# A residual quantiser with depthwise convolutions: three small operations of a stage go from VectorE to GpSimd, score tiles hold eight groups in shared PSUM tiles, and DMA transposes and adding DMAs take strict turns

## The chip, the cores and the metric

The kernel runs on one core of a Trainium2 chip. The metric is the device time of one execution in microseconds (us). The engines are named as in the profile: PE (TensorE), DVE (VectorE), ACT (ScalarE), POOL (GpSimd) and SP (SyncE, which here only issues transfers). A "q" behind the name (POOLq, SPq) means the engine's instruction queue issuing a transfer or waiting.

## The reference

The input x has 2 sequences of 16000 tokens with 512 channels, in bf16. A depthwise convolution with three taps and a SiLU give z. Four rounds of residual quantisation follow, each with a code book of 8 words, and the sum of the chosen words goes through a second depthwise convolution.

```python
for i in range(K):                      # K = 3 taps
    z = z + xp[:, i:i+T, :] * dw_enc[i]
z = silu(z)
res, q = z, 0
for s in range(4):                      # four code books of 8 words
    cb = codebooks[s]
    d2 = sum(res*res)[..., None] - 2.0 * einsum("btd,cd->btc", res, cb) + sum(cb*cb)
    sel = cb[d2.argmin(-1)]
    q, res = q + sel, res - sel
for i in range(K):
    y = y + qp[:, i:i+T, :] * dw_dec[i]
```

## The kernel before

The 32000 tokens are laid out as 128 partitions by 250 groups: group g holds one token of each partition. The groups are worked on in 16 chunks (`SIZES`: one of 12, fourteen of 16, one of 14, which is padded to 16). Channels lie on the partitions in four blocks of 128, tokens along the free dimension.

**Loading.** The rows of chunk 0 come in with a plain transfer (L291) into the third residual buffer, PE transposes them into `ps_x` (L454), and ACT and DVE move two blocks each to `XT` (L459, L461). All later chunks come in with DMA transposes issued by SP, up to four groups each (L486). `XT` has two buffers.

**Front** (`front`, four blocks a chunk): DVE makes the three tap products Z and T (L553). They are added on DVE (L561) or, for most, by a DMA that POOL issues and that adds T onto Z on its way (L559, 75 of them). SiLU takes an exponential (L565), plus one on DVE (L569), a logarithm (L573), another exponential (L576), all three on ACT, and a product on DVE (L581) that writes the residual tile RES.

**Four stages** (`stage`), each in this order:
- PE writes a mask (L637) and then the products of RES with itself and with the code words (L643) into a PSUM score tile. In the kernel before a tile `PS` is one bank with up to six groups, from a pool `psG` of two.
- DVE takes each token's squared norm out of the tile with a maximum (L651, `norm`) and copies the dots with the eight words (L654, `dots`).
- DVE adds the norm (L673, `with_norm`), adds the words' own norms (L679, `distance`) and puts a rank into the low half of each key so that the first of equal words wins (L684, `ranks`).
- DVE takes the least key (L689) and makes a one-hot pattern (L697). PE transposes it (L707), and DVE copies it out (L714).
- Except in the last stage, the chosen word is taken off the residual in eight parts: on PE and DVE (`SEL` L731, L747) or on PE and ACT (`NEW` L752 and L731, L758). How many of the four channel blocks go to DVE in stages 0, 1 and 2 stands in `ON_DVE`; each block is two parts.

**Output** (`finish`, `outputs`): the decoder is a product of one-hot patterns with tables of words times taps (`Y`, L785); ACT copies it out (L791) and SP stores it (L795).

The other PSUM tiles (`ps_oh`, `SEL`, `NEW`, `Y`) come from a pool `psA` of three tiles with two banks each. The three residual buffers, key buffers and one-hot buffers set how many chunks are under way.

**Order.** The order of the instructions is made by a planner (`Plan`): each task has an engine, a time for which it holds that engine, a time until its result is there, needs, a due time and the buffers it takes and gives. `ROUNDS` holds seeds and numbers of forward and backward passes. Tasks are written out in the order of their planned starts, so each engine's queue follows the plan and runs strictly in that order. Into planned idle time of PE the planner puts matmuls without use (`warm`, L430; `WARM` is the share of busy time it aims for), which keep PE's clock up. Transposes and adding DMAs have the planner's engine "DMA". In the program, `keep_apart` makes each wait for an earlier one of the other kind:

```python
if len(others) >= LAG:
    tc.add_manual_dep(t.ins, others[-LAG].name, ...)
```

The adds' wait stands in POOL's queue, the transposes' in SP's.

Of the kernel before, what the change touches and what calls it, by code (L numbers as in the profile page):

```python
# [21 lines left out]
GB = 6  # L22
# [6 lines left out]
ON_DVE = [(1, 2, 2)]  # L29
# [3 lines left out]
WARM = 0.6  # L33
# [4 lines left out]

RUN = 4

AHEAD = 40

# [4 lines left out]
ROUNDS = [(940, 0.3, 0.0, 7), (4101, 0.3, 2.0, 9), (5991, 0.3, 0.0, 7), (15520, 0.3, 0.0, 10)]  # L47
# [6 lines left out]
APART, CLUMP = 0.5, 2.0  # L54

LAG = 2


class Plan:
# [18 lines left out]
    def pass_over(self, rank, backward=False):  # L78
# [20 lines left out]
        while True:  # L99
            going = True  # L100
            while going:
                going = False
                for e in engines:
# [3 lines left out]
                    while e == "DMA" and ready[e]:  # L107
                        at, n = heapq.heappop(ready[e])
                        passed.append((at, n))
                        if all(slots[k] > 0 for k in tasks[n][takes]):  # L110
                            kind, lost = tasks[n][8][0], 0.0
                            if kind and sort and kind != sort:
                                lost = max(0.0, APART - (now - ended))
                            if pick is None or at + CLUMP * lost < least:
                                pick, least, gap = n, at + CLUMP * lost, lost
# [62 lines left out]
    def emit(self, starts, order):  # L178
        tasks = self.tasks
        free, back, spans, end = self.slots["psG"], [], [], 0.0  # L180
        for n in order:
            engine, hold, delay, _, _, emit, take, give, _, _ = tasks[n]
            at = starts[n]
            if engine == "PE":
                while end + 0.3 <= at:
# [3 lines left out]
                    while spans and spans[0][1] < end - 4.0:  # L189
                        spans.pop(0)  # L190
                    if free > 0 and sum(b - max(a, end - 4.0) for a, b in spans) < 4.0 * WARM and self.idle():
                        spans.append((end, end + 0.3))
                        end += 0.3
                    else:
                        end += 0.1
# [5 lines left out]
            free -= take.count("psG")  # L201
            for _ in range(give.count("psG")):
                heapq.heappush(back, at + max(hold, delay))
# [4 lines left out]
def kernel(  # L208
# [32 lines left out]
    psG = ctx.enter_context(tc.tile_pool(name="psG", bufs=2, space=bass.MemoryType.PSUM))  # L241
    psA = ctx.enter_context(tc.tile_pool(name="psA", bufs=3, space=bass.MemoryType.PSUM))
# [25 lines left out]
    def tap_columns():  # L268
        pst = psA.tile([P, 2, 512], F32, name="ps_w", tag="psa")
# [6 lines left out]
    plan = Plan({"XT": 2, "Z": ZB, "T": TB, "E": EB, "LN": LNB, "Y": YB, "psG": 2, "psA": 3, "RES": 3, "KEY": 3,  # L276
# [14 lines left out]
    nc.sync.dma_start(out=XR[:, 1:G + 2, :], in_=xv[:, 0:G + 1, :])  # L291
    for b in range(B):
        p = b * HB
        nc.scalar.dma_start(out=XR[p + 1:p + HB, 0, :], in_=xv[p:p + HB - 1, S - 1, :])
# [4 lines left out]
    def code_words():  # L299
        pst = psA.tile([P, 2, 512], F32, name="ps_cbt", tag="psa")  # L300
# [13 lines left out]
    def code_norms():  # L314
# [12 lines left out]
        psg = psA.tile([P, 2, 512], F32, name="ps_g", tag="psa")  # L327
# [69 lines left out]
    ident, book = landed(1.8), landed(9.3)  # L397
    taps_in = setup(0.2, 0.4, [ident, landed(3.0)], early, tap_columns)
# [24 lines left out]
    pending = []  # L423

    def warm():
        if not scored[2:]:
            return False
        if not pending:
            pending.append(psG.tile([P, 512], F32, name="PS"))
        nc.tensor.matmul(pending[0][:, 0:GB * HT].rearrange("p (r c) -> p r c", c=HT), lhsT=IDENT, rhs=MASK, start=True, stop=True,  # L430
                         skip_group_check=True)
# [4 lines left out]
    def ahead():  # L436
        pending.append(psG.tile([P, 512], F32, name="PS"))
        for _ in range(AHEAD):
            nc.tensor.matmul(pending[0][:, 0:P], lhsT=IDENT, rhs=IDENT, start=True, stop=True, skip_group_check=True)

    plan.add("PE", 0.1 * AHEAD, 0.1 * AHEAD, [taps_in], early, ahead)

    def load_rows(st, org):
# [6 lines left out]
        def turn(i):  # L450
            pst = psA.tile([P, 2, 512], F32, name="ps_x", tag="psa")
            st["ps", i] = pst.rearrange("p b n -> p (b n)").bitcast(BF16)
            for n in range(G + 2):
                nc.tensor.transpose(st["ps", i][:, n * P:(n + 1) * P], XR[:, n, i * P:(i + 1) * P], IDENT)  # L454

        def move(i):
            src = st["ps", i][:, 0:(G + 2) * P].rearrange("p (n t) -> p n t", t=P)
            if i % 2:
# [4 lines left out]
        rows = st["rows"] = plan.add("LOAD", 0.0, 1.2 + 0.46 * (G + 2), [], early, room, take=("XT",))  # L463
        for i in range(KT):
            t = plan.add("PE", 0.11 * (G + 2), 0.11 * (G + 2) + 0.2, [rows, ident], early, lambda i=i: turn(i),
                         take=("psA",))
            cost = (0.11, 0.07)[i % 2] * (G + 2)
            st["moved", i] = plan.add(("ACT", "DVE")[i % 2], cost, cost + 0.2, [t], early, lambda i=i: move(i), give=("psA",))
# [4 lines left out]
    def load(st, org):  # L473
# [29 lines left out]
        def behind():  # L503
            nc.gpsimd.tensor_copy(st["XT"][0:1, 0, 0, 0:2], XR[0:1, 1, 0:2])
# [10 lines left out]
        for n in range(0, G + 2, RUN):  # L515
            due = org - 2.2 * PERIOD + 0.01 * n
            m = min(RUN, inside - n)
            if m > 0:
                done.append(plan.add("DMA", 0.7 * m, 2.7 + 0.7 * m, [room], due, lambda n=n, m=m: run(n, m), mode=RUNS))
# [94 lines left out]
    def stage(st, s, due):  # L614
# [14 lines left out]
        def score(q, m):  # L629
# [4 lines left out]
            PS = pending.pop() if pending else psG.tile([P, 512], F32, name="PS")  # L634
            V = u["V", q] = PS[:, 0:m * (hi - lo)].rearrange("p (r c) -> p r c", r=m)
            for h in range(2):
                nc.tensor.matmul(V[h * HT:(h + 1) * HT, :, own:own + HT], lhsT=IDENT[:, h * HT:(h + 1) * HT], rhs=MASK[:, 0:m, :],  # L637
                                 start=True, stop=False, skip_group_check=True)
            for r in range(m):
                for i in range(KT):  # L640
                    for h in range(2):
                        half = RES[:, i, 2 * (q + r) + h, :]
                        nc.tensor.matmul(V[h * HT:(h + 1) * HT, r, :], lhsT=half[:, LC:LC + HT], rhs=half[:, lo:hi],  # L643
# [6 lines left out]
        def norm(q, m):  # L650
            nc.vector.tensor_reduce(out=u["TR"][:, q:q + m], in_=u["V", q][:, :, own:own + HT], axis=AX.X, op=ALU.max)  # L651

        def dots(q, m):
            nc.vector.tensor_copy(u["PR"][:, q:q + m, :], u["V", q][:, :, pick:pick + C])  # L654

        banks = -(-G // GB)
        q = 0
        for n in range(banks):
            m = -(-(G - q) // (banks - n))
# [4 lines left out]
            t = plan.add("PE", 0.175 * m, 0.175 * m + 0.25, needs, due, lambda q=q, m=m: score(q, m), take=("psG",), mode=(COLUMNS, COLUMNS, 0, 0.0),  # L664
# [3 lines left out]
            maxima.append(plan.add("DVE", 0.06 + 0.01 * m, 0.2, [maxima[-1]], due, lambda q=q, m=m: dots(q, m), give=("psG",)))  # L668
            q += m

        def with_norm():
            u["V"] = small.tile([P, GC, C], BF16, name="V")
            nc.vector.tensor_tensor(out=u["V"][:, 0:G, :], in0=u["PR"][:, 0:G, :], in1=u["TR"][:, 0:G].to_broadcast([P, G, C]),  # L673
                                    op=ALU.add)

        def distance():
            u["KEY"] = free["KEY"].pop(0)
            g2 = GPOS[:, C * s:C * s + C].rearrange("p (o c) -> p o c", o=1).to_broadcast([P, G, C])
            nc.vector.tensor_tensor(out=u["KEY"][1][:, 0:G, :, 1], in0=u["V"][:, 0:G, :], in1=g2, op=ALU.add)  # L679

        def ranks():

            word = u["KEY"][1]
            nc.vector.scalar_tensor_tensor(out=word[:, 0:G, :, 0], in0=word[:, 0:G, :, 1], scalar=0.0,  # L684
# [17 lines left out]
        def turn():  # L702

            pst = psA.tile([P, 2, 512], F32, name="ps_oh", tag="psa")
# [13 lines left out]
        t = plan.add("DVE", 0.2, 0.33, maxima, due, with_norm)  # L718
        t = plan.add("DVE", 0.2, 0.33, [t] + preset[0:3], due, distance, take=("KEY",))
        t = plan.add("DVE", 0.2, 0.33, [t], due, ranks)  # L720
# [19 lines left out]
        def chosen(i, j):  # L740
            SEL = u["SEL", i, j] = psA.tile([P, 2, 512], F32, name="SEL", tag="psa")
# [7 lines left out]
        def rest(i, j):  # L749
            NEW = u["NEW", i, j] = psA.tile([P, 2, 512], F32, name="NEW", tag="psa")  # L750
# [22 lines left out]

    kept = {}

    def outputs(groups, needs, due):
# [4 lines left out]
        def decode(k):  # L781
            Y = u[k] = psA.tile([P, 2, D], F32, name="Y", tag="psa")
# [107 lines left out]
```

## Time and profile before

| | |
|---|---|
| time, median of 3 runs | 745.02 us (744.42 to 745.52) |
| the profiled execution | 742.04 us |
| its span | 740.3 us |
| mean granted clock of PE | 0.934 |
| busiest engines | DVE 93%, ACT 90%, PE 80% of the span |
| POOL | 11% of the span |
| DMA queues, share of 16 engines | 39.5% (issued by SP and ACT), 29.9% (by POOL) |

The span runs from the program's first instruction to the end of its last; the rest of the profiled execution's time lies around it. Busy times are of one execution. A group's mean is the duration of one instruction; where instructions of an engine overlap, the next one starts before the mean has passed. "Idle before" is the time in which the engine waited for such an instruction, and the name behind the arrow is what ended most of it.

### The profile page before, as it was taken

Reading aid. Unit: us, or ns where it says so; the run is one execution under the profiler, and the core shown is the slowest. Engines: PE = TensorE matmul, PEld = TensorE weight load, DVE = VectorE, ACT = ScalarE, POOL = GpSimd, SP = SyncE. Lnnn points to the kernel's source line nnn. Section 1 sums busy time; section 2 is a strip of 40 time slices with the busy share of each in tenths; the row PEclk is TensorE's granted clock in tenths of the full one; section 3 lists DMA queues with packets and bytes.
Section 4 is the critical chain, followed back from the end, with each engine's and each line's share of the span. In section 5 each row is a group of like instructions: output and inputs, shape, how many; then the busy total and the mean of one; then the engine's idle time right before and its main releaser. Section 6 shows DMA issues by size and latency. Waiting matters only on the chain. (4 is left out here: it accounts for less than half of the span.)

```text
span 740.3 us, 23586 instructions
## 1 busy us (share of the span) xinstructions
PE 590.8 (80%) x10478; PEld 314.2 (42%) x10544; DVE 685.9 (93%) x1359; ACT 665.4 (90%) x539; POOL 81.7 (11%) x104
## 2 busy tenths in 40 slices
PE   5037687787987888986978888878988898989996
PEld 5023334344444444434444444444453444444543
DVE  6999989899999999997999999989999999998952
ACT  2688979899999999998899999989999999976576
POOL 3112101111101011100101111100111101100000
PEclk9566969999999999999799899999999999999999
DMA  7969795859696967839978875959896435320234
GB/s 178 189 130 182 135 200 104 141 122 201 182 174 158 209 133 164 165 116 143 188 171 177 175 165 143 182 132 174 172 210 136 131 64 152 87 88 2 88 143 199
DMA packets 160833, 111.14 MB, mean 150 GB/s; under 512 B 142426, under 2 KB 142811, under 8 KB 160603
## 3 DMA queue, kind: packets, MB, share of 16 engines
q1 hardware_dynamic: 148976, 69.61, 39.5%
q0 software_dynamic: 11472, 39.76, 29.9%
q8 instruction: 82, 1.34, 0.8%
q10 hardware_dynamic: 282, 0.26, 0.1%
q14 instruction: 21, 0.16, 0.1%
HBM read 2.39 MB, written 32.77 MB: 47 GB/s over the span
## 5 line engine op out<-in xcount | busy, mean ns | idle before, releaser
L758 ACT ACTIVATE RES<-NEW 128x1024 bf16<-128x1024 f32 (+1 forms) x218 | 218.5, 1043 | 28.6 <-PE NEW L731 21.9
L747 DVE TENSOR_TENSOR RES<-RES,SEL 128x1024 bf16<-128x1024 bf16 (+1 forms) x166 | 197.5, 1203 | 6.7 <-PE SEL L731 6.3
L643 PE MATMUL PS<-RES 128*64 128x80 bf16 (+1 forms) x8064 | 176.1, 203 | 11.2 <-DVE RES L581 9.7
L643 PEld LDWEIGHTS <-RES 128*64 128x64 bf16 x8064 | 172.8, 115 | 19.6 <-DVE RES L581 10.6
L752 PE MATMUL NEW<-RES,IDENT 128*128 128x512 bf16 (+1 forms) x436 | 137.7, 399 | 31.3 <-ACT RES L758 15.6
L791 ACT ACTIVATE YSB<-Y 128x1024 bf16<-128x1024 f32 (+1 forms) x126 | 126.6, 1061 | 8.4 <-PE Y L785 4.5
L565 ACT ACTIVATE E<-Z 128x2048 bf16<-128x2048 bf16 (+1 forms) x64 | 123.2, 1931 | 11.5 <-DMA Z<-T 4.0
L559 POOL DMA_DIRECT2D Z<-T x75 | 72.9, 976 | 537.5 <-ACT RES L758 78.8
L573 ACT ACTIVATE LN<-E 128x2048 f32<-128x2048 bf16 (+1 forms) x64 | 123.0, 1923 | 9.9 <-DVE E L569 9.2
L576 ACT ACTIVATE E<-LN 128x2048 bf16<-128x2048 f32 (+1 forms) x64 | 123.0, 1922 | 0.4
L651 DVE TENSOR_REDUCE TR<-PS 128x5 bf16<-128x320 f32 (+1 forms) x188 | 96.0, 515 | 14.4 <-PE PS L643 14.3
L553 DVE TENSOR_SCALAR T<-XT,WENC 128x2048 bf16<-128x2048 bf16 (+1 forms) x128 | 94.8, 745 | 5.1 <-DMA Z<-T 5.1
L731 PEld LDWEIGHTS <-CBN 32*128 32x128 bf16 x768 | 32.6, 92 | 137.7 <-issue 134.3
L785 PE MATMUL Y<-A,OHT 128*128 128x512 bf16 x219 | 77.6, 382 | 16.4 <-ACT RES L758 6.0
L731 PE MATMUL NEW<-OHT,CBN 32*128 32x512 bf16 (+1 forms) x436 | 88.3, 402 | 0.1
L581 DVE TENSOR_TENSOR RES<-Z,E 128x2048 bf16<-128x2048 bf16 (+1 forms) x64 | 77.3, 1208 | 0.0
L731 PE MATMUL SEL<-OHT,CBN 32*128 32x512 bf16 (+1 forms) x332 | 58.7, 396 | 22.0 <-ACT RES L758 13.3
L637 PE MATMUL PS<-MASK,IDENT 128*64 128x320 bf16 (+1 forms) x376 | 64.6, 340 | 8.6 <-DVE PR L654 6.2
L561 DVE TENSOR_TENSOR Z<-Z,T 128x2048 bf16<-128x2048 bf16 (+1 forms) x53 | 62.5, 1181 | 2.7 <-DMA Z<-T 2.7
L752 PEld LDWEIGHTS <-IDENT 128*128 128x128 bf16 x436 | 33.1, 99 | 67.4 <-issue 57.4
L430 PE MATMUL PS<-MASK,IDENT 128*128 128x384 bf16 x167 | 46.2, 359 | 10.1 <-DVE PR L654 9.8
L785 PEld LDWEIGHTS <-OHT 128*128 128x128 bf16 x373 | 32.1, 97 | 50.8 <-issue 22.8
(78 smaller groups left out, 416.2 us busy)
## 6 DMA issues: line engine op xcount, KB each, us to landing
Z<-T POOLq DMA_DIRECT2D x75, 512.0 KB, 5.6
out_dram<-YSB SPq DMA_DIRECT2D x61, 512.0 KB, 3.2
RES<-in_x_dram SPq DMA_DIRECT2D x1, 1664.0 KB, 6.8
XT<-in_x_dram SPq DMA_TRANSPOSE x74, 5.7
out_dram<-YSB SPq DMA_DIRECT2D x1, 384.0 KB, 2.3
out_dram<-YSB SPq DMA_DIRECT2D x1, 256.0 KB, 2.7
A<-in_dw_dec_dram POOLq DMA_DIRECT2D x2, 96.0 KB, 6.4
CB<-in_codebooks_dram ACTq DMA_DIRECT2D x1, 128.0 KB
```

Of the source, the lines that this page charges most:

```text
L553: nc.vector.tensor_scalar(out=places(u[name]), in0=taps(i, k), scalar1=WENC[:, i, k:k + 1], scalar2=None, op0=ALU.mult)
L565: nc.scalar.activation(u["E"][:, 0:G, :], u["Z"][:, 0:G, :], ACT.Exp, scale=-1.0)
L573: nc.scalar.activation(u["LN"][:, 0:G, :], u["E"][:, 0:G, :], ACT.Ln)
L576: nc.scalar.activation(u["E"][:, 0:G, :], u["LN"][:, 0:G, :], ACT.Exp, scale=-1.0)
L643: nc.tensor.matmul(V[h * HT:(h + 1) * HT, r, :], lhsT=half[:, LC:LC + HT], rhs=half[:, lo:hi], start=False, stop=(i == KT - 1), skip_group ...
L651: nc.vector.tensor_reduce(out=u["TR"][:, q:q + m], in_=u["V", q][:, :, own:own + HT], axis=AX.X, op=ALU.max)
L731: nc.tensor.matmul(ps, lhsT=CBN[s][rows, i * P:(i + 1) * P], rhs=u["OHT"][rows, 0:MB, :], start=start, stop=True, skip_group_check=True)
L747: nc.vector.tensor_tensor(out=old, in0=old, in1=u["SEL", i, j][:, :, 0:W].rearrange("p h (m t) -> p h m t", t=HT), op=ALU.add)
L752: nc.tensor.matmul(NEW[:, h, 0:W], lhsT=IDENT, rhs=tokens(i, j + h, 1), start=True, stop=False, skip_group_check=True)
L758: nc.scalar.activation(old, u["NEW", i, j][:, :, 0:W].rearrange("p h (m t) -> p h m t", t=HT), ACT.Copy)
L785: nc.tensor.matmul(Y[:, h, :], lhsT=lhs(), rhs=rhs, start=(a == 0), stop=(a == len(terms) - 1))
L791: nc.scalar.activation(u["YSB"][:, k:k + n, :], u[k][:, 0:n, :], ACT.Copy)
```

## The change

Seven things change together.

1. `with_norm`, `distance` and `ranks` go to POOL in all four stages. `ranks` becomes two instructions there.
2. `GB` goes from 6 to 4, counted for one bank; a score tile is now a double tile of two banks with up to eight groups, written and read as `[:, b, ...]`. The pool `psG` is gone: `psA` has four double tiles, which all users take through `bank`.
3. `ON_DVE` takes turns between (2, 2, 2) and (1, 2, 2).
4. `LAG` is 1: a transpose waits for the last add before it, and an add for the last transpose. The planner's gap between kinds goes from 0.5 to 1.9 or 2.3 us.
5. At the start, the rows of chunk 0 come in with two transfers, all from SP's queue, and PE's transposes of a block go in two parts; one block is moved by DVE and three by ACT. The matmuls ahead of the work (`ahead`) no longer wait for the taps.
6. The warm-up matmuls have 512 columns of code words, use a `psA` tile, and come only ahead of a task that takes such a tile; the planner's parameters for them change.
7. The planner's estimates and seeds (`ROUNDS`) are new, so the order differs everywhere. In the built program DVE has 180 subtractions L747 for 166, 128 reductions and 128 copies of dots for 188 each; ACT has 204 updates for 218; PE has 85 warm-up matmuls for 167. Transposes and adds change places 65 times for 53. POOL has 256 more instructions.

Line numbers are those of the kernel before.

```diff
-GB = 6
+GB = 4
-ON_DVE = [(1, 2, 2)]
+ON_DVE = [(2, 2, 2), (1, 2, 2)]
-WARM = 0.6
+WARM, WINDOW, TICK = 0.75, 3.4, 0.22
+ON_POOL = (0, 1, 2, 3)
+POOL_SMALL = (0.45, 0.65)
-ROUNDS = [(940, 0.3, 0.0, 7), (4101, 0.3, 2.0, 9), (5991, 0.3, 0.0, 7), (15520, 0.3, 0.0, 10)]
+ROUNDS = [(734, 1.0, 0.0, 9), (2861, 0.3, 0.0, 2), (4622, 0.3, 0.0, 3)]
-APART, CLUMP = 0.5, 2.0
-LAG = 2
+APART = (0.0, 1.9, 2.3)
+CLUMP = 2.0
+LAG = 1
...
-    psG = ctx.enter_context(tc.tile_pool(name="psG", bufs=2, space=bass.MemoryType.PSUM))
-    psA = ctx.enter_context(tc.tile_pool(name="psA", bufs=3, space=bass.MemoryType.PSUM))
+    psA = ctx.enter_context(tc.tile_pool(name="psA", bufs=4, space=bass.MemoryType.PSUM))
+    pending = []
+    def bank(name):
+        return pending.pop() if pending else psA.tile([P, 2, 512], F32, name=name, tag="psa")
...
-    nc.sync.dma_start(out=XR[:, 1:G + 2, :], in_=xv[:, 0:G + 1, :])
     for b in range(B):
         p = b * HB
-        nc.scalar.dma_start(out=XR[p + 1:p + HB, 0, :], in_=xv[p:p + HB - 1, S - 1, :])
+        nc.sync.dma_start(out=XR[p + 1:p + HB, 0, :], in_=xv[p:p + HB - 1, S - 1, :])
+    HALF = (G + 2) // 2
+    for a, b in ((1, HALF), (HALF, G + 2)):
+        nc.sync.dma_start(out=XR[:, a:b, :], in_=xv[:, a - 1:b - 1, :])
...
     def warm():
...
-        nc.tensor.matmul(pending[0][:, 0:GB * HT].rearrange("p (r c) -> p r c", c=HT), lhsT=IDENT, rhs=MASK, ...)
+        nc.tensor.matmul(pending[0][:, 0, :], lhsT=IDENT, rhs=CB4, ...)
...
     def score(q, m):
...
-            V = u["V", q] = PS[:, 0:m * (hi - lo)].rearrange("p (r c) -> p r c", r=m)
-            for h in range(2):
-                nc.tensor.matmul(V[h * HT:(h + 1) * HT, :, own:own + HT], lhsT=IDENT[:, h * HT:(h + 1) * HT], rhs=MASK[:, 0:m, :],
-                                 start=True, stop=False, skip_group_check=True)
+            V = u["V", q] = PS[:, :, 0:m // 2 * (hi - lo)].rearrange("p b (r c) -> p b r c", c=hi - lo)
+            for b in range(2):
+                for h in range(2):
+                    nc.tensor.matmul(V[h * HT:(h + 1) * HT, b, :, own:own + HT], lhsT=IDENT[:, h * HT:(h + 1) * HT],
+                                     rhs=MASK[:, 0:m // 2, :], start=True, stop=False, skip_group_check=True)
...
-        banks = -(-G // GB)
+        banks = -(-G // (2 * GB))
...
     def with_norm():
-            nc.vector.tensor_tensor(out=u["V"][:, 0:G, :], in0=u["PR"][:, 0:G, :], in1=u["TR"][:, 0:G].to_broadcast([P, G, C]),
+            small_on(s).tensor_tensor(out=u["V"][:, 0:G, :], in0=u["PR"][:, 0:G, :], in1=u["TR"][:, 0:G].to_broadcast([P, G, C]),
...
     def distance():
-            nc.vector.tensor_tensor(out=u["KEY"][1][:, 0:G, :, 1], in0=u["V"][:, 0:G, :], in1=g2, op=ALU.add)
+            small_on(s).tensor_tensor(out=u["KEY"][1][:, 0:G, :, 1], in0=u["V"][:, 0:G, :], in1=g2, op=ALU.add)
...
     def ranks():
             word = u["KEY"][1]
+            if s in ON_POOL:
+                nc.gpsimd.tensor_scalar(out=u["V"][:, 0:G, :], in0=word[:, 0:G, :, 1], scalar1=0.0, scalar2=None, op0=ALU.is_lt)
+                nc.gpsimd.tensor_tensor(out=word[:, 0:G, :, 0], in0=u["V"][:, 0:G, :], in1=RANK.to_broadcast([P, G, C]), op=ALU.subtract)
+                return
...
+    def small_on(s):
+        return nc.gpsimd if s in ON_POOL else nc.vector
```

102 lines of the change are left out of this document (52 added, 50 removed).

## The prediction

> **What bounds the kernel now.** I began with the page's first part and the busy time of each engine by stretch, because a kernel with a pipeline of 16 chunks has a filling, a steady and an emptying part with different limits.
>
> ```profile
> PE 590.8 (80%) x10478; PEld 314.2 (42%) x10544; DVE 685.9 (93%) x1359; ACT 665.4 (90%) x539; POOL 81.7 (11%) x104
> ```
>
> ```profile
> 100.00:200.00 100.00, 82.18 (x1533) 42.20 (x1538) 94.85 (x185) 94.66 (x76) 11.68 (x12) 0.95 0.78 154
> 200.00:300.00 100.00, 83.38 (x1537) 43.53 (x1544) 99.43 (x196) 99.94 (x81) 10.33 (x11) 0.99 0.80 170
> 300.00:400.00 100.00, 84.31 (x1486) 44.18 (x1496) 94.24 (x186) 93.96 (x77) 10.69 (x12) 0.94 0.79 156
> ...
> 660.00:680.00 20.00, 19.09 (x373) 9.45 (x365) 17.97 (x35) 11.61 (x12) 0.00 (x0) 1.00 0.08 29
> ```
>
> The columns are the stretch, its length, then busy us (and instructions) of PE, PEld, DVE, ACT and POOL, the granted TensorE clock, the DMA share and GB/s. From 100 to 640 us (six rows, three shown) DVE is busy 522.8 and ACT 522.0 of 540 us, both 97%: two engines bound the middle together, and relieving one alone gains nothing. POOL does 11%. From 0 to 60 us ACT is only 60% busy while DVE is full from 20 us on (19.4 and 19.8 of 20): DVE sets the start. From 660 us on PE is at 95%: the emptying part belongs to PE and to the chain through one chunk's stages.
>
> Next, the groups by form, for prices.
>
> ```profile
> L758 ACT ACTIVATE RES<-NEW 128x1024 bf16<-128x1024 f32 x204 | 207.6, 1060 | 27.4 <-PE NEW L731 20.8 <-PE SEL L731 6.5
> L747 DVE TENSOR_TENSOR RES<-RES,SEL 128x1024 bf16<-128x1024 bf16 x156 | 188.4, 1219 | 6.4 <-PE SEL L731 6.3
> L651 DVE TENSOR_REDUCE TR<-PS 128x5 bf16<-128x320 f32 x120 | 58.6, 492 | 8.2 <-PE PS L643 8.1
> L651 DVE TENSOR_REDUCE TR<-PS 128x6 bf16<-128x384 f32 x68 | 37.8, 556 | 6.3 <-PE PS L643 6.2
> L679 DVE TENSOR_TENSOR KEY<-V,GPOS 128x128 bf16<-128x128 bf16 x60 | 18.2, 304 | 0.2
> L684 DVE SCALAR_TENSOR_TENSOR KEY<-KEY,RANK 128x128 bf16<-128x128 bf16 x60 | 18.2, 303 | 0.2
> L673 DVE TENSOR_TENSOR V<-PR,TR 128x128 bf16<-128x128 bf16 x60 | 17.5, 291 | 0.2
> ```
>
> These means are too large as prices on a full engine, since each instruction starts before the last has ended. DVE's timeline shows it (start, duration):
>
> ```profile
> 317.81 0.31 DVE L679 TENSOR_TENSOR KEY<-V,GPOS 128x128 bf16<-128x128 bf16 x1
> 318.00 0.50 DVE L651 TENSOR_REDUCE TR<-PS 128x5 bf16<-128x320 f32 x1
> 318.40 0.31 DVE L684 SCALAR_TENSOR_TENSOR KEY<-KEY,RANK 128x128 bf16<-128x128 bf16 x1
> 318.60 0.77 DVE L553 TENSOR_SCALAR T<-XT,WENC 128x2048 bf16<-128x2048 bf16 x1
> ```
>
> From start to start a small operation takes 0.20 us, not 0.30, and a five-group reduction 0.40. Read the same way, a six-group reduction takes 0.46, a copy of its dots 0.11 to 0.12, a subtraction L747 1.13, and an ACT update L758 0.91.
>
> **The change part by part.** The sum is made against the profiled execution: 742.04 us, a span of 740.3 and 1.7 around it. The median of the runs, 745.02, is 3.0 above it.
>
> *Small operations to POOL.* L673, L679 and L684 leave DVE in all 64 stages: 64 x 3 x 0.20 = 38.4 us. POOL gets four instructions for them (the compare and subtract become two). POOL has no such two-input operation in this trace. Nearest rows: the copy L496 of 508 columns takes 610 ns, a copy of two columns (L504) 174, so 0.86 ns per column: one input of 128 columns costs 0.28 us, and a second input at most as much per column again, 0.39. I take 3 x 0.39 + 0.28 = 1.45, with three handovers 1.6 us (bounds 1.1 to 3.0). That is 64 x 1.6 = 102 us on an engine with 82. In the middle it hides: from the start of L673 to the start of L689 DVE now takes 3.2 us at the median of 64 stages, because other work stands between. Where only one chunk is left, the three take 1.0 us (725.75 to 726.75 in the chain), so there it adds 0.6 a stage.
>
> *Eight groups to a score tile.* Sixty stages of 16 groups go from tiles of 6, 5 and 5 to two of 8. Per 64 columns a reduction costs 0.067 more, so 512 columns take 0.60. Before: 0.46 + 2 x 0.40 + 0.34 for three copies = 1.60; after: 2 x (0.60 + 0.13) = 1.46. That saves 60 x 0.14 = 8.4 us of DVE. PE's masks go from six of 0.13 to 0.16 to eight of 256 columns, about even.
>
> *Stage 0 of seven chunks.* Two updates each move from ACT to DVE: 14 on DVE at 1.13 = +15.8, 14 off ACT at 0.91 (two of them shorter) = -12.3.
>
> *DVE's net* is -38.4 - 8.4 + 15.8 = -31 us, ACT's -12.3. What POOL takes from DVE must be set against that. The trace has one event:
>
> ```profile
> 556.75 0.61 POOL L496 COPY XT<-XE 128x508 bf16<-128x508 bf16 x1 [13.38 <-DMA XE<-in_x_dram]
> 556.81 0.11 PEld L752 LDWEIGHTS <-IDENT 128*128 128x128 bf16 x2 [0.23 <-issue]
> 556.81 0.60 PE L752 MATMUL NEW<-RES,IDENT 128*128 128x512 bf16 x2
> 557.01 1.43 DVE L581 TENSOR_TENSOR RES<-Z,E 128x2048 bf16<-128x2048 bf16 x1
> ```
>
> This L581 ran beside POOL's copy and took 1.43 us; the 60 of its form have a median of 1.22. So POOL reading costs DVE up to 0.21 us. L561, L581 and L697, with two inputs in SBUF, and L553 and L569, the fast one-input form (2048 columns in 0.66 us), make 307 us from start to start, 47% of what DVE would have left. With POOL's shorter instructions: 256 x 0.47 x 0.21 x 0.39/0.61 = 16 us (bounds 0 and 256 x 0.21 = 54). DVE is then at -15, ACT at -12. At the 97% of the middle the smaller decides: **-12 us**.
>
> The Trainium skill, SBUF — State Buffer, section "Who interferes with whom", speaks against this part: VectorE with two SBUF inputs or in a two-port mode shares a port pair with GpSimd, and whichever comes second is blocked for the whole instruction. The event agrees in kind (0.21 us lost of at most 0.35 us shared); by the full rule the loss goes towards the upper bound, and the sum to the second rival below.
>
> *Transposes and adds never together.* Each now waits for the last of the other kind instead of the last but one, and they change places 65 times instead of 53 in the built order. An add takes 5.6 us to land, a transpose 5.7 (DMA issues), so 12 more turns are at most 68 us of transfer time. I cost it at nothing: the cover is two chunk buffers, some 45 us ahead; gone, a turn costs up to 5.7 us. On the other side, the longest stall of the middle is a late add:
>
> ```profile
> 345.82 0.75 DVE L553 TENSOR_SCALAR T<-XT,WENC 128x2048 bf16<-128x2048 bf16 x1 [4.21 <-DMA Z<-T]
> ```
>
> That add was issued at 333.5 with transposes in flight and landed after 12.3 us; the PE clock then fell to half from 349.6 to 359.8. If adds fly alone this should go: **-3 us** (bounds +10 and -8).
>
> *Start.* DVE is the limit until 60 us. The code norms (33.6 to 35.4, in the full stretch) move into DVE's wait for the code book (5.6 us idle before 11.2), and one copy of 1.08 us goes to ACT: **-3 us** (-4 to 0). Half loads of the rows gain little, as PE's transposes now stand behind the norms' matmul, which needs the book landed at 8.6.
>
> *Shared PSUM tiles, warm-up matmuls* (85 of 512 columns for 167 of 384): PE waits for score tiles 16 us now (L430 9.8 and L637 6.2, released by DVE's PR) and may wait as much for the four shared ones; PE has 16% idle in the middle, so **0** (-5 to +10; without the cover the clock falls more often).
>
> *Tail:* PE's work is unchanged; the last two stages show the longer POOL chain: 2 x 0.6 = **+1** (0 to +4).
>
> Sum: 742 - 12 - 3 - 3 + 1 = **725 us** profiled, **728 us** as a median.
>
> **The rivals.** *One, both engines close up.* DVE keeps more slack than ACT and stops starving it; most of ACT's 18 us idle in the middle goes: 728 - 16 = 712 us. For it: 200 to 300 us runs at 99.9% without any disturbance. Against: the disturbances are PE's clock and transfers, which the change doesn't remove surely.
>
> *Two, POOL takes DVE's time: slower.* Its place is DVE's instructions beside POOL's. At the upper price DVE stands at -31 + 54 = +23, becomes the sole bound, and the time is 742 + 23 - 3 + 3 = 765 us. It decides when DVE loses over 31 us, 0.12 us for each of 256 instructions. For it: the one event; the Trainium skill's rule on the shared ports, named above, would bring it about. Against: POOL's descriptor writing (L559) lengthened beside L553 (0.86 us to 1.2 and more) while L553 did not (754 ns beside it, 751 apart).
>
> *Three, the queue of POOL: slower.* In the built order 41 of 64 stage chains stand right behind an add, and 22 of those adds wait for a transpose; today only adds would be late, then the stage too, and behind it DVE's L689, PE and the next score. If each of 22 is held 3.4 us, 75 us of chain; with three chunks in flight a third shows: 728 + 25 = 753 us. For it: POOL's adds already sit 12 to 17 us in waits. Against: those waits are for their own data, in the planned order.
>
> **How the numbers follow.** The forecast (717 to 738) gets 0.48, rival one 0.22, two 0.16 with half of it between 742 and 765, three 0.12, and 0.02 for anything else. A range of 708 to 752 leaves out a little of rival one and about half of two and three. A measurement here tells 0.2% (1.5 us) from no change: faster 0.74 (forecast, rival one, a mild form of two), same 0.04, slower 0.22.
>
> **What would show it.** Right: DVE's busy time near 670, ACT's near 654, both about 97% in the middle; the small operations on POOL at 0.3 to 0.4 us; L553, L561 and L581 no longer than by 0.1 us at the mean. Wrong: L581 or L553 means up by 0.2 us (rival two); L689 waiting long for POOL with an add ahead in POOL's queue (rival three); more half-clock stretches of PE (shared tiles); L553 or L565 waiting for Z<-T (turns of the transfers).

## The result, and the profile after

The changed kernel takes 789.31 us (median of 4 runs, 786.98 to 790.71), the kernel before in the same series 745.27 us. The ratio is 1.058, 95% interval 1.054 to 1.062: slower by 5.8%, where 728 us was forecast. The profiled execution has a span of 788.1 us, before 740.3. All times and ratios of this document are of undisturbed runs; f4, g3, h1 and i3 below had slower, disturbed ones as well.

Line numbers are now those of the changed kernel (L559 before is L571 now, and so on): L497 issues the transposes, L571 the adds. L565 makes the tap products, L573 adds them on DVE, L593 writes RES, L656 makes the scores, L664 and L667 are `norm` and `dots`. On POOL, L686 is `with_norm`, L692 `distance`, L698 and L699 the two halves of `ranks`. L706 takes the least key, L714 makes the one-hot pattern and L724 transposes it; L749 with L765 or with L770 and L776 are the updates by `SEL` and by `NEW`. First the page's busy times, the line that answers to the first one shown of before:

```profile
PE 599.2 (76%) x10570; PEld 325.3 (41%) x10570; DVE 665.5 (84%) x1056; ACT 657.2 (83%) x526; POOL 231.6 (29%) x361
```

DVE and ACT have as much to do as forecast (670 and 654). What is new is idle time, as the busy time by stretch shows (columns as before):

```profile
100.00:200.00 100.00, 75.23 (x1296) 39.24 (x1296) 86.66 (x140) 83.33 (x66) 32.56 (x48) 0.88 0.72 140
200.00:300.00 100.00, 76.09 (x1331) 43.17 (x1330) 87.86 (x133) 91.36 (x74) 29.82 (x43) 0.86 0.78 166
300.00:400.00 100.00, 79.90 (x1491) 42.69 (x1492) 91.40 (x141) 91.60 (x74) 31.07 (x46) 0.91 0.70 156
```

DVE was at 94 to 99 in these rows. Busy plus idle time of one engine is the span, so DVE's ledger tells where +47.9 us come from: busy -20.4 (685.9 to 665.5), idle in the first 60 us +7.1 (7.6 to 14.7), idle in the middle +52.0 (18.4 to 70.4; the middle is from 60 us to 100 us before the end), idle in the last 100 us +9.2 (28.4 to 37.6). By what ended it, DVE's idle time in the middle is 32.0 for POOL's keys (before none), 20.1 for scores (before 3.3) and 10.0 for added tiles (before 7.7). The waits say the same of the whole span (total us, times, longest):

```profile
POOL V L686 <- DVE PR L667: 299.2, 50, 14.8
POOL Z L571 <- DMA XT<-in_x_dram: 52.7, 13, 12.7
DVE M L706 <- POOL KEY L699: 43.1, 33, 4.4
DVE TR L664 <- PE PS L656: 30.4, 37, 2.7
PE SEL L749 <- DVE PR L667: 9.8, 10, 4.9
SPq L497 <- DMA Z<-T: 324.1, 31, 17.8
```

What is new: DVE waits for POOL before it takes the least key (L706); POOL's adds (L571) wait for a transpose 13 times by this view, where it was once (7.9 us); and PE's `SEL` waits for the reader of a score tile (L667), which could not happen with two pools. SP's transposes wait 324 us for adds, before 100.7.

One passage of the timeline shows a POOL operation beside DVE, and an add ahead of a stage in POOL's queue (start, duration, then in brackets the idle time before and its releaser):

```profile
616.52 1.22 DVE L573 TENSOR_TENSOR Z<-Z,T 128x2048 bf16<-128x2048 bf16 x1
616.69 1.31 POOL L686 TENSOR_TENSOR V<-PR,TR 128x128 bf16<-128x128 bf16 x1 [7.04 <-DVE PR L667]
...
621.72 0.89 POOL L571 DMA_DIRECT2D Z<-T  x1 [3.72 <-ACT E L577]
...
622.34 0.71 POOL L692 TENSOR_TENSOR KEY<-V,GPOS 128x128 bf16<-128x128 bf16 x1
...
623.13 0.52 POOL L698 TENSOR_SCALAR V<-KEY 128x128 bf16<-128x128 bf16 x1
...
623.74 0.40 POOL L699 TENSOR_TENSOR KEY<-V,RANK 128x128 bf16<-128x128 bf16 x1
...
624.17 0.29 DVE L706 TENSOR_REDUCE M<-KEY 128x16 f32<-128x128 f32 x1 [3.96 <-POOL KEY L699]
...
625.38 0.61 PE L724 MATMUL ps_oh<-IDENT,OH 128*128 128x128 bf16 x4 [3.88 <-DVE OH L714]
...
628.10 1.02 ACT L776 ACTIVATE RES<-NEW 128x1024 bf16<-128x1024 f32 x1 [4.00 <-PE SEL L749]
```

L686 begins beside DVE's L573 and takes 1.31 us; L699, with no such neighbour, takes 0.40. Between L686 and L692 an add stands in POOL's queue, and POOL sat idle for 3.72 us before it. So L692, whose input was there at 618.0, starts at 622.3. DVE, PE and ACT each stand still for about 4 us behind it, one after the other.

The bracket at 621.72 names the wrong cause. The trace also keeps the waits of POOL's queue one by one, and there the add's wait for a transpose, issued at 616.48 and landed at 621.18, ended at 621.21; the exponential L577 merely ended next. Counted by these records, 30 of the 75 adds waited for a transpose to land, before 7.

### The profile page after: what moved, and what is told of

Same layout as the page of the kernel before. It is cut to its first block, busy times and chain, and to the rows that moved or that the text cites. A ratio compares the mean times of both kernels' runs of the same rounds, so it can differ in the third digit from the quotient of the medians.

```text
span 788.1 us, 23619 instructions
## 1 busy us (share of the span) xinstructions
PE 599.2 (76%) x10570; PEld 325.3 (41%) x10570; DVE 665.5 (84%) x1056; ACT 657.2 (83%) x526; POOL 231.6 (29%) x361
## 4 chain that ended last, share of the span: by engine, by line
PE 23%; DVE 22%; ACT 21%; DMA 14%; POOL 9%; issue 7%; SPq 3%; POOLq 0%; ACTq 0%; DVEq 0%
PE PS L656 8%; DMA Z<-T 7%; DVE RES L765 6%; DMA XT<-in_x_dram 6%; ACT RES L776 5%; PE NEW L770 5%; ACT E L577 4%; ACT YSB L812 4%; ACT LN L585 4%; PE Y L806 4%; ACT E L588 4%; DVE T L565 3%; PE NEW L749 3%; SPq L497 3%; DVE TR L664 3%
## 5 line engine op out<-in xcount | busy, mean ns | idle before, releaser
L776 ACT ACTIVATE RES<-NEW 128x1024 bf16<-128x1024 f32 (+1 forms) x200 | 196.5, 1019 | 43.3 <-PE NEW L749 26.3
L765 DVE TENSOR_TENSOR RES<-RES,SEL 128x1024 bf16<-128x1024 bf16 (+1 forms) x180 | 210.1, 1195 | 8.5 <-PE SEL L749 8.1
L656 PE MATMUL PS<-RES 128*64 128x72 bf16 (+1 forms) x8064 | 181.9, 210 | 32.2 <-DVE RES L593 25.7
L656 PEld LDWEIGHTS <-RES 128*64 128x64 bf16 x8064 | 180.1, 122 | 35.6 <-DVE RES L593 26.4
L770 PE MATMUL NEW<-RES,IDENT 128*128 128x512 bf16 (+1 forms) x400 | 135.0, 423 | 29.1 <-ACT RES L776 11.7
L812 ACT ACTIVATE YSB<-Y 128x1024 bf16<-128x1024 f32 x125 | 122.7, 1027 | 25.4 <-PE Y L806 15.9
L571 POOL DMA_DIRECT2D Z<-T x75 | 71.5, 973 | 217.5 <-DMA XT<-in_x_dram 52.7
L577 ACT ACTIVATE E<-Z 128x2048 bf16<-128x2048 bf16 (+1 forms) x64 | 120.7, 1889 | 17.0 <-DVE Z L573 10.9
L686 POOL TENSOR_TENSOR V<-PR,TR 128x128 bf16<-128x128 bf16 (+1 forms) x64 | 45.6, 713 | 299.3 <-DVE PR L667 299.2
L664 DVE TENSOR_REDUCE TR<-PS 128x8 bf16<-128x512 f32 (+1 forms) x128 | 86.4, 677 | 30.6 <-PE PS L656 30.4
L806 PE MATMUL Y<-A,OHT 128*128 128x512 bf16 x247 | 88.5, 410 | 15.0 <-ACT RES L776 3.8
L565 DVE TENSOR_SCALAR T<-XT,WENC 128x2048 bf16<-128x2048 bf16 (+1 forms) x128 | 94.8, 747 | 2.5 <-DMA Z<-T 2.3
L749 PEld LDWEIGHTS <-CBN 32*128 32x128 bf16 x768 | 30.5, 92 | 158.9 <-issue 144.2
L749 PE MATMUL SEL<-OHT,CBN 32*128 32x512 bf16 (+1 forms) x360 | 63.8, 406 | 32.6 <-ACT RES L776 11.0
L749 PE MATMUL NEW<-OHT,CBN 32*128 32x512 bf16 (+1 forms) x400 | 84.9, 421 | 1.9 <-DVE OHT L731 1.8
L593 DVE TENSOR_TENSOR RES<-Z,E 128x2048 bf16<-128x2048 bf16 (+1 forms) x64 | 78.4, 1226 | 0.5 <-ACT E L588 0.4
L573 DVE TENSOR_TENSOR Z<-Z,T 128x2048 bf16<-128x2048 bf16 (+1 forms) x53 | 63.2, 1195 | 8.4 <-DMA Z<-T 8.4
L650 PE MATMUL PS<-MASK,IDENT 128*64 128x256 bf16 (+1 forms) x512 | 57.3, 306 | 11.0 <-DVE RES L765 6.2
L770 PEld LDWEIGHTS <-IDENT 128*128 128x128 bf16 x408 | 30.3, 101 | 78.4 <-issue 66.1
```

Of the source, the lines that this page charges most:

```text
L565: nc.vector.tensor_scalar(out=places(u[name]), in0=taps(i, k), scalar1=WENC[:, i, k:k + 1], scalar2=None, op0=ALU.mult)
L577: nc.scalar.activation(u["E"][:, 0:G, :], u["Z"][:, 0:G, :], ACT.Exp, scale=-1.0)
L656: nc.tensor.matmul(V[h * HT:(h + 1) * HT, r // (m // 2), r % (m // 2), :], lhsT=half[:, LC:LC + HT], rhs=half[:, lo:hi], start=False, stop ...
L664: nc.vector.tensor_reduce(out=u["TR"][:, q:q + m].rearrange("p (b r) -> p b r", b=2), in_=u["V", q][:, :, :, own:own + HT], axis=AX.X, op= ...
L749: nc.tensor.matmul(ps, lhsT=CBN[s][rows, i * P:(i + 1) * P], rhs=u["OHT"][rows, 0:MB, :], start=start, stop=True, skip_group_check=True)
L765: nc.vector.tensor_tensor(out=old, in0=old, in1=u["SEL", i, j][:, :, 0:W].rearrange("p h (m t) -> p h m t", t=HT), op=ALU.add)
```

## The experiments

"Chip" is the median, "ratio" that to the kernel before in the same series (740 to 744 us), with its 95% interval. "Plan's end" is the length that the kernel's own planner gives to its order, from its own prices, while the program is built. It is no measurement; it serves to compare how far the chip falls behind orders that the planner thinks equally good. The comparison of one pool with two is rough, since the changed kernel's planner also prices a group of a transpose at 0.6 us for 0.7.

**The small operations' engine, and the turns, in the order of the changed kernel.**

```diff
 e1:  def small_on(s):
-    return nc.gpsimd if s in ON_POOL else nc.vector
+    return nc.vector              # and ranks as one DVE instruction
 e2:
-LAG = 1
+LAG = 2
 e3: both
```

> The changed kernel with the same order of instructions on every engine, but with_norm, distance and ranks issued on DVE at the places where POOL's stood. Theory POOL (the small operations on POOL are slow beside DVE and are held behind adds in POOL's queue): the waits of DVE's L706 for POOL (36 us) and what follows from them go, PE's mean clock rises from 0.87 to over 0.90, DVE is busy about 665 + 38 = 703 us; as DVE becomes fuller the time falls to 755 to 770 us. Theory turns (transposes and adds that exclude each other): 785 to 800 us. Theory clock (fewer warm-up matmuls, shared PSUM tiles): PE's clock stays under 0.88 and the time at 780 to 800 us.

> The changed kernel with LAG 2 as before: same order, but a transpose waits for the last add but one, and an add for the last transpose but one. Theory turns: POOL's wait of 53 us for transposes goes, and the time falls by 20 us or more, to 768 or less. Theory POOL: adds stand shorter at the head of POOL's queue, so some 10 us, 775 to 782. Theory clock: no change, 785 to 793.

> Both edits together on the changed kernel. If POOL and turns are separate causes their gains add up (for instance -25 and -20 give 744). If the turns cost only through POOL's queue, this equals the small operations on DVE alone to within 5 us. Theory clock: 780 or more.

Measured: e1 778.2 us (1.048, 1.040 to 1.056), e2 772.3 (1.039, 1.031 to 1.047), e3 772.5 (1.041, 1.031 to 1.050). By the ratios (0.01 is 7.4 us) taking the operations off POOL gives 8 us back with turns of 1 and nothing with turns of 2; looser turns give 14 with the operations on POOL and 5 without. Each interval is about 0.008 to either side, so the 14 is clear of noise, the 8 barely and the 5 not. So by the kernel's time about 14 of 43 us come back.

This understates the two, because e1 and e3 also give DVE its work back (busy 699.0 and 698.9 us for 665.5). DVE's idle time over the whole span is the fairer measure: 54.4 us before, 122.6 in the changed kernel, 107.1 in e2, 83.5 in e1 and 65.9 in e3. Without the two parts 57 of the 68 us of added idle time are gone, in an order that is otherwise the same (about 51 by e3's median, which lies 6 us above its profiled execution). Of the 24.5 us by which e3's span still exceeds that of before, 13.0 are work: DVE is busy longer than before, since among other things the stage 0 updates stay on it.

In e2 DVE waits for POOL's key less, though still:

```profile
DVE M L706 <- POOL KEY L699: 27.4, 35, 2.6
```

**Only the small operations, in the order of the kernel before.**

```diff
-            nc.vector.tensor_tensor(out=u["V"]..., nc.vector.tensor_tensor(out=u["KEY"]..., nc.vector.scalar_tensor_tensor(...)
+            nc.gpsimd.tensor_tensor(...), nc.gpsimd.tensor_tensor(...), nc.gpsimd.tensor_scalar(...), nc.gpsimd.tensor_tensor(...)
```

> The kernel before with its own order, PSUM tiles, LAG 2 and warm-up, but with_norm, distance and ranks issued on POOL where DVE's stood. Theory POOL: DVE's busy time falls by 38 us, yet L689 waits for POOL and the time rises to 765 to 790 us. Theories turns and clock: POOL is harmless, and the time is 725 to 748 us.

Measured: 754.8 us (1.016, 1.009 to 1.023). Lines are those of the kernel before; L685 is the second half of `ranks`. DVE's busy time falls by 30.0 (685.9 to 655.9), and its idle time rises by more: +32.5 in the middle, +9.8 in the last 100 us.

```profile
DVE M L689 <- POOL KEY L685: 33.8, 31, 3.8
```

There are no tighter turns and no shared tiles here. The time taken off DVE came back as waiting, 33.8 us of it for POOL's key: the median time from the start of L673 to the end of the last key operation went from 2.43 to 3.00 us, from the start of L673 to that of L689 from 3.18 to 3.90.

**The clock.** The granted clock of PE is 0.868, before 0.934; half clock takes 26% of the middle, before 10%. Four matmuls without use were put ahead of each one-hot transposition, where PE waits.

```diff
             pst = bank("ps_oh")
+            for _ in range(4):
+                nc.tensor.matmul(pst[:, 1, :], lhsT=IDENT, rhs=CB4, start=True, stop=True, skip_group_check=True)
```

> The changed kernel with four more matmuls without use (512 columns, into the unused second bank of the tile) ahead of each of the 64 transpositions of the one-hot pattern, where PE often waits for DVE; nothing else changes. Theory clock (PE's half-clock stretches, 24% of the middle against 9% before, are a cause of their own): the half-clock share falls under 15%, and the time by 15 us or more, to 773 or less. Theory symptom (the clock only shows that PE waits): the share falls, but the time stays within 5 us of 789 or rises by the added PE work, at most 64 x 4 x 0.22 = 56 us.

Measured: 787.2 us (1.059, 1.054 to 1.064) at a clock of 0.905. Half clock still takes 17% of the middle. Over half of the clock came back and no time. This alone doesn't settle it: the added matmuls also stand in the way of the transposition, which starts 1.60 us after its one-hot pattern at the median, for 0.57 in the changed kernel, and that can have used up a gain. What speaks against the clock as the cause is e1 and e3, where most of DVE's added idle time is gone at a clock as low as ever (0.849 and 0.869).

**The order by itself.** f3 is the kernel before with the changed kernel's `ROUNDS`; f2 the changed kernel with all put back except the shared tiles, the eight-group score tile and the start (so the old `ROUNDS` too; the warm-up matmuls have 512 columns and use shared tiles); f4 the changed kernel with small operations planned and run on DVE, LAG 2 and the old gap. Each gets an order that nobody chose for it.

> The kernel before with only the seeds and passes of the planner (ROUNDS) of the changed kernel. Theory order (a plan's luck is worth several per cent): 755 us or more. All other theories: within 5 us of before, 738 to 750.

> The changed kernel with all but the shared double PSUM tiles, the eight-group score tiles and the start put back: small operations planned and issued on DVE, LAG 2 and the old gap, the old share of stages on DVE, the old warm-up rule (it now uses shared tiles), the old seeds. Theory tiles (sharing and larger score tiles make DVE and ACT wait for PE): 760 us or more, DVE's wait for PS over 15 us against 3. Theory order (the plan's seeds and due times): near 745 to 755. Theory POOL and turns alone: 735 to 748.

> The changed kernel with the small operations planned and issued on DVE, LAG 2 and the old gap between transposes and adds, so that the planner knows of it; tiles, shares of DVE, warm-up and seeds as changed. If POOL and turns cost through a plan that did not fit (772 us with the changed order kept), this falls to 750 or less; theory tiles or order: it stays at 760 to 785.

Measured: f3 784.7 (1.054, 1.049 to 1.060), f2 809.2 (1.090, 1.082 to 1.097), f4 811.8 (1.092, 1.082 to 1.101). Other seeds alone cost the kernel before 5.4%. A version with an order not chosen for it therefore says little, and from here on each got seeds drawn for it, by the plan's end.

**Orders drawn for each version.** g1: the changed kernel with LAG 2, the old gap, `POOL_SMALL = (0.9, 1.1)` and new `ROUNDS`. g2: the changed kernel with new `ROUNDS` alone. g3: the kernel before with small operations planned on POOL at 0.9 us and new `ROUNDS`. g4: the kernel before with new `ROUNDS` alone.

> The changed kernel with LAG 2 and the old gap of 0.5 us between turns in the plan, the plan's price of a pool instruction raised from 0.45 to 0.9 us (what the trace shows beside VectorE), and ROUNDS drawn anew by the plan's own end, which is 714.5 us (715.5 for the changed kernel, 729.6 for the kernel before; these are the planner's own sums, made while the program is built). So far the chip came 15 and 29 us behind the plan with two PSUM pools (745 and 785 us) and 58 to 74 us with one. Theory 'order': the changed kernel lost its time to an order drawn for prices that the chip does not keep; with true prices and the turns kept at 2 the chip follows within 30 us: 730 to 745. Theory 'one pool': four tiles for all make every late reader hold up the next PE work whatever the order; the chip comes 45 us or more behind: 760 or more.

> The changed kernel with nothing but other ROUNDS; plan's own end 720.7 us (715.5 in the changed kernel). Theory 'order by luck' (this one draw was bad): 740 to 765. Theory 'the configuration' (turns of one, pool chain priced at half, one pool): the same lag behind the plan as the changed kernel, 785 to 800.

> The kernel before with the small stage instructions on the pool engine and planned there at 0.9 us each, ROUNDS drawn anew; plan's own end 724.2 us; two PSUM pools and turns of 2 as before. Theory 'pool instructions help once the plan knows their price': 15 to 29 us behind the plan, 739 to 753, VectorE busy near 656. Theory 'the pool chain is on the path in any order': as the unplanned one, 755 or more, with VectorE waiting for the pool engine's KEY over 25 us.

> The kernel before with nothing but other ROUNDS, drawn by the plan's own end in the same way; plan's own end 727.9 us (729.6 in the kernel before). Control for the three above. If the plan's end tells the chip's time for two pools within 15 to 29 us: 743 to 757. If the order of the kernel before was a lucky one on the chip itself: 760 to 785, which would take the plan's end away as a yardstick.

Measured: g1 766.1 (1.034, 1.029 to 1.040), g2 801.5 (1.080, 1.073 to 1.088), g3 767.4 (1.038, 1.030 to 1.046), g4 758.2 (1.024, 1.017 to 1.030). g2 speaks against one unlucky draw in the changed kernel: 81 us behind its plan, as against 74. The true price takes away most of DVE's wait for keys in g1:

```profile
DVE M L706 <- POOL KEY L699: 6.6, 7, 2.2
PE SEL L749 <- DVE PR L667: 6.6, 6, 2.2
PE NEW L770 <- DVE PR L667: 6.6, 5, 2.5
DVE TR L664 <- PE PS L656: 39.8, 43, 2.9
```

What remains is DVE waiting for scores (25.1 us in the middle). g3 has the same wait (25.5), and DVE has more idle time for late adds there (23.1 for 8.2 in g4); that POOL's operations now stand ahead of the adds may be why, but wasn't tested. It came out at neither forecast's mechanism: DVE waits only 2.5 us for the key in the middle, and yet it is some 11 us slower than g4 by the ratios, and g4's plan is the longer by 3.7.

**One pool or two, and the size of the score tile.** h1: the shared tiles, the eight-group tile and the start of the changed kernel, small operations on DVE, LAG 2, new `ROUNDS`. h2: the same with `GB = 3`, so at most six groups to a tile.

> The changed kernel's four shared double tiles with eight groups to a score tile and its start, and all else as in the kernel before (small stage instructions on VectorE, turns of 2, its warm-up rule, one pair of adds), with ROUNDS drawn by the plan's own end as in the two-pool control: 720.9 us (control 727.9, which took 758 on the chip, 30 behind). Theory 'one pool': 50 us or more behind the plan, 771 to 785, and PE's SEL and NEW work found waiting for a score tile's reader on VectorE (line of PR), which two pools cannot show. Theory 'one pool costs nothing once its order is drawn': 745 to 755.

> As h1, but with at most six groups to a score tile, as the kernel before has (GB = 3), ROUNDS drawn for it, plan's own end 728.9 us. If the eight-group tile is what costs (a longer score before VectorE may begin): 30 us behind the plan, 755 to 762. If the sharing costs: 50 or more behind, 778 to 790.

Measured: h1 777.1 (1.047, 1.035 to 1.059), h2 798.3 (1.074, 1.066 to 1.082). Six groups are no better in their own order, so nothing here puts the cost on the eight-group tile. All versions with a plan's end, in us:

| kernel | PSUM pools | small operations | turns | plan's end | chip | behind |
|---|---|---|---|---|---|---|
| before (these series) | two | DVE | 2 | 729.6 | 742 | 12 |
| f3 | two | DVE | 2 | 755.3 | 784.7 | 29 |
| g4 | two | DVE | 2 | 727.9 | 758.2 | 30 |
| g3 | two | POOL, 0.9 | 2 | 724.2 | 767.4 | 43 |
| f2 | one | DVE | 2 | 750.6 | 809.2 | 59 |
| h1 | one | DVE | 2 | 720.9 | 777.1 | 56 |
| h2, six groups | one | DVE | 2 | 728.9 | 798.3 | 69 |
| f4 | one | DVE | 2 | 761.5 | 811.8 | 50 |
| g1 | one | POOL, 0.9 | 2 | 714.5 | 766.1 | 52 |
| after | one | POOL, 0.45 | 1 | 715.5 | 789.3 | 74 |
| g2 | one | POOL, 0.45 | 1 | 720.7 | 801.5 | 81 |

With small operations on DVE, one pool falls 20 to 40 us further behind than the new orders with two (f3, g4). A sign of it is PE idle at work that takes a tile whose last reader belongs to the other sort, score tiles against all others. With two pools this can't occur, and it is 0.0 us in the middle of before, f3, g3 and g4; it is 28.6 in the changed kernel, 25.0 in g1, 23.2 in f2, 25.9 in h2. This is idle time of PE, which is not the fullest engine, and not time of the kernel. With small operations on POOL one pool and two are only 8 us apart (g3, g1), so the two costs do not add.

**The turns.** h4 is the kernel before with LAG 1, i3 with LAG 3, i99 with LAG 99 (no turns), all in its own order; h3 is g1 with LAG 1 in the order of g1.

```diff
 h4, i3, i99:
-LAG = 2
+LAG = 1, 3 and 99
```

> The kernel before with LAG 1 and nothing else, in its own order, no small instruction on the pool engine. Theory 'turns cost through the pool queue's small instructions': nearly nothing here, 740 to 748 beside 742. Theory 'turns delay the transfers themselves': 752 to 765, with VectorE and ScalarE waiting for the adds' tiles.

> The changed kernel with the pool instructions priced at 0.9 us and ROUNDS drawn anew (766 us with LAG 2), with LAG back at 1 and the order the same. Theory 'turns hold the pool queue's adds and so the small instructions behind them': 776 to 786, VectorE waiting for the pool engine's KEY 15 us or more (4 us with LAG 2). If the turns only mattered in the badly priced order: within 4 us of 766.

> The kernel before with turns of 3 in its own order; the third point of a series (turns of 1: 779 us, of 2: 742). Theory 'a turn holds the pool queue's adds behind a transposition, and SyncE's transpositions behind an add': SyncE's wait for adds was 264 us at 1 and 101 us at 2; at 3 it falls under 50 us, the waits of VectorE and ScalarE for added tiles fall from 12 us in the middle to some 8, and the time goes to 736 to 742. Theory 'turns of 2 are where transfers begin to hold each other up': adds take longer to land than 5.6 us and the time goes to 745 to 765.

> The kernel before with the turns taken out altogether (each transposition and add goes when its own data and buffers are ready). First theory: 734 to 742, as turns of 3. Second theory: adds and transpositions run together and the adds land late, 750 to 790, with VectorE and ScalarE waiting more than 20 us for added tiles.

Measured: h4 778.9 (1.050, 1.042 to 1.057), h3 813.5 (1.096, 1.088 to 1.103), i3 744.0 (1.0005, 0.997 to 1.004), i99 746.0 (1.006, 1.002 to 1.010). The theory that turns act only through POOL's small operations fell with h4: 37 us without any of them. The waits of h4, SP's queue first:

```profile
SPq L486 <- DMA Z<-T: 264.0, 28, 19.7
POOL Z L559 <- DMA XT<-in_x_dram: 60.9, 6, 13.0
```

and of i3:

```profile
SPq L486 <- DMA Z<-T: 22.2, 7, 6.7
```

An add lands in 5.2 us in h4, in 5.6 before and 6.0 in i99, so tight turns shorten the transfers and lose the time ahead of them. DVE and ACT stand idle 43.8 us in the middle of h4 for added tiles (31.9 and 11.9), before 11.7. Turns of 2 are loose enough: nothing is gained beyond. In the changed kernel, whose order was planned with a gap of 1.9 to 2.3 us for a turn, LAG 1 costs 14 us (e2); in an order made without that gap it costs 37 (h4) and 46 (h3).

## Why the prediction was wrong

**Busy times: right.** DVE 665.5 for 670, ACT 657.2 for 654. The parts fit less well: for the small operations and what POOL takes together, e4 shows -30.0 us where the sum had -38.4 + 16 = -22.

**"At the 97% of the middle the smaller decides": the step that failed.** -12 us took for granted that an order planned for shorter queues would be kept as tightly as the old one. DVE ran at 87 to 91% in the three rows shown. Its busy time fell by 20.4 us and its idle time rose by 68, of which 52.0 in the middle: 44 us were lost where 12 were to be won. Most of that idle time goes when the small operations leave POOL and the turns are loose again (e3); these are the terms that the sum had at nothing.

**"In the middle it hides": wrong, and the chain was mis-sized.** The chain on POOL was taken at 1.6 us (bounds 1.1 to 3.0) under a cover of 3.2. From the start of L686 to the end of L699 it takes 2.87 us at the median and over 4.9 in one stage of ten. Alone the four operations take 0.40, 0.40, 0.53 and 0.40, which with handovers is near the estimate. The means are longer (last two numbers: total us, ns of one):

```profile
L698 POOL TENSOR_SCALAR V<-KEY 128x128 bf16<-128x128 bf16 x60 | 41.8, 696 | 4.8
L686 POOL TENSOR_TENSOR V<-PR,TR 128x128 bf16<-128x128 bf16 x60 | 41.5, 691 | 284.5 <-DVE PR L667 284.4
L692 POOL TENSOR_TENSOR KEY<-V,GPOS 128x128 bf16<-128x128 bf16 x60 | 33.2, 554 | 4.4
L699 POOL TENSOR_TENSOR KEY<-V,RANK 128x128 bf16<-128x128 bf16 x60 | 29.1, 486 | 5.0
L706 DVE TENSOR_REDUCE M<-KEY 128x16 f32<-128x128 f32 x60 | 16.9, 281 | 36.2 <-POOL KEY L699 36.2
```

The cover was no slack. The order of DVE's queue put L689 where its key would be ready, and a key that comes later (by 0.57 us at the median in e4) stops the whole queue there, 31 times in 64 stages: e4, in the old order, lost 13 us where 30 of DVE's work were taken away.

**What POOL takes from DVE, 16 us: the direction was wrong.** It is mostly POOL that loses: sixty chains keep it busy for 145.6 us, and at the durations alone would for 104. Beside a two-input DVE operation its median goes from 0.40 to 1.30 (L686), from 0.53 to 1.37 (L698); DVE's L593 goes from 1.217 to 1.291 at the mean, L565 from 0.747 to 0.799, and L765, with one input in PSUM, stays at 1.213. Over all conflicting instructions DVE loses some 5 us (35 x 0.052 + 13 x 0.051 + 9 x 0.101 + 22 x 0.074 + 6 x 0.075). So rival two fell. The Trainium skill, SBUF — State Buffer, section "Who interferes with whom", has VectorE and GpSimd hold the shared port pair against each other; the trace agrees: beside L765, whose second input is in PSUM, POOL's operations keep their 0.40 (L686, L692, L699) and 0.53 us (L698) at the median. That POOL loses more may come from DVE's queue having hardly a gap; this wasn't tested.

**Rival three (0.12, 753 us): the mechanism was there.** Adds with waits of their own stood ahead of stage operations in POOL's queue, at 621.72 one that had waited for a transpose. By the trace one of a stage's four operations is held over 0.2 us behind an add in 20 of 64 stages, 41 us together, and in 14 of them (33 us) the add had waited for a transpose; the rival had 22 stages and 75 us. Of the 43.1 us for which DVE waits for keys, 30 fall in such stages. In e2 no operation is held behind an add that waited for a transpose, and looser turns gave back 14 us where the rival had 25. Its sign of recognition, "L689 waiting long for POOL with an add ahead", is L706 in the passage shown.

**Turns at nothing: wrong in the cover.** "Two chunk buffers, some 45 us ahead" cover the transposes. An add that waits for a transpose has no such cover, since DVE or ACT takes its tile soon after; and POOL stood idle ahead of such an add not "up to 5.7 us" but up to 12.7 (13.0 in h4). The late-add stall that was to give -3 did not go: idle for added tiles is 15.5 us in the middle (DVE 10.0, ACT 5.5), before 11.7.

**Shared tiles 0 (-5 to +10): mis-sized.** The trace of before could have shown that PE waits for tiles; not that two kinds of readers, each late for its own reasons, would hold up each other's work. One pool falls 20 to 40 us further behind its plan where small operations and turns are as before. The start differs there too, and every order, so this is a difference between drawn orders and not an edit by itself. In the changed kernel's own order it can't be that much: e3, with one pool, has only 12 us more DVE idle time than before (17 by its median). The sign named, more half-clock stretches, came; it stays in e1 and e3, where most of the idle time goes.

**Start and tail.** -3 became +7.1 of DVE idle in the first 60 us, and +1 became +9.2 in the last 100. For the tail e4, with POOL alone, shows +9.8; no run takes the start apart.

**Still open:** why DVE waits some 20 to 33 us for scores in nearly all new orders, with one pool and with two (g3 25.5, f3 20.5, but g4 3.9 and before 3.3). Open too is why the kernel before is only 12 us behind its plan, when the other orders of the same version are 29 and 30 behind; an order chosen for its measured time would look like this, and nothing on record tells how it was chosen. No version here beats it; turns of 3 equal it.

## What to carry to other kernels

Count busy and idle time of a bound engine separately: an edit priced by its instructions moves the first, and in a queue with a fixed order the second can grow by more. A step handed to an engine whose queue also issues transfers waits for whatever those transfers wait for, so its price is that of the queue, not of the instruction. Before an added wait is costed at nothing, name the cover for each of the two sides that it holds back, not only for the one with deep buffers.

## What the runs showed of the hardware

A short POOL operation of 128 columns took 0.40 to 0.53 us alone and 0.7 to 1.4 at the median beside a two-input DVE operation, while the DVE operation grew by 0.07 to 0.10 us at the mean. PE's granted clock rose from 0.868 to 0.905 with idle matmuls, and the time stayed (787.2 and 789.3 us), while the transposition behind those matmuls came later. Adds and transposes let loose together (i99) landed in 6.0 and 6.6 us, for 5.6 and 5.7 with turns of 2 and 5.2 and 4.6 in strict turns (h4); the kernel's time with them let loose is 0.6% above that with turns of 2.
